# Turning u by transposing DMAs in place of TensorE transposes, in a fused attention and MLP kernel

## The chip, the core and the metric

The kernel runs on one core of a Trainium2 chip. The metric is the device time of one execution in microseconds (us); lower is better. The engines are named as in the profile: PE is TensorE (matmuls; its weight loads are listed as PEld), DVE is VectorE, ACT is ScalarE, POOL is GpSimd, SP is SyncE, which here only issues DMAs. POOL and ACT can issue DMAs as well.

## The reference

Inputs are q, k, v of shape (4, 8, 768, 64) and an 8x8 sort net per batch and head. After five rounds of normalising the sort net's rows and columns, keys and values are mixed between blocks of 96 tokens, attention runs inside each block, and a residual MLP of two stages follows on x (4, 768, 512):

```python
attn = softmax(scale * q_b @ k_sorted_b.T)          # inside each block
x = (attn @ v_sorted_b) as (batch, seq, 512)
a1 = alpha1 * x + beta1
tok = np.einsum('ts,bsd->btd', w_tok, a1)
u = x + lam * tok
a2 = alpha2 * u + beta2
ch = np.maximum(a2 @ w_ch1, 0.0) @ w_ch2            # 512 -> 2048 -> 512
return u + lam * ch
```

The change touches the line `a2 = alpha2 * u + beta2` and what feeds it.

## The kernel before

The order on every engine is written out by hand (`manual_schedule`); each engine runs its own instructions strictly in that order, and semaphores connect them. Per batch the 768 tokens are six tiles of 128 (kt 0 to 5), in two halves of three tiles (384 tokens). The 512 columns are four blocks of 128 (ci), the hidden 2048 are sixteen blocks (m).

`token_mix(b, kt)` does one token tile: six matmuls with the transposed `w_tok` into a psM bank (line 589), then u = x + rb on POOL (597), where rb is the row part (row sum of `w_tok` times beta1·lam), t = psum · alpha1·lam on DVE (601) and u += t on DVE (602). `row_part` (575 to 579) makes rb once, during batch 0: tile 0 on DVE, tile 1 on ACT, tiles 2 to 5 on POOL, one after each POOL u.

A copy of each u tile to bf16 (`u16`, ACT, line 603) is put in the list `late`; `tick()` runs such an entry at the second tick after it was entered, and `tick(True)` runs all at once. `weave` ticks once after each step of its main stream.

The channel MLP wants u with its columns on the partitions. `u_turn(b, half, ci)` (614 to 627) makes one of the 8 pieces per batch: three TensorE transposes of u16 into a PSUM bank (619), and an ACT activation that evicts it with alpha2 and beta2 as scale and bias (625) to a bf16 tile `a2T` [128, 384]. `hidden(b, half)` takes them: for each m four matmuls (635) and a relu, on DVE for every fourth m (643), else on ACT (645). `result(b, half, kk)` makes one output tile with sixteen matmuls (672), two DVE instructions (681, 682) and the store from SP (683).

PSUM: psM has three banks, shared by mixing, turns, hidden and result; psX has one (also used by a part of the turns); psA has two double banks for attention and for the preparation of keys, queries and values.

The stages for each batch b, n being the next batch: `both` is hidden(b, 0), three results of half 0 and hidden(b, 1), woven with `attention(n)`. `join` is, alternating, the mixing of batch n's tiles and the results of half 1 of batch b, woven with `ahead(n + 1)`, which prepares values (with a relay through DRAM, SP lines 412 and 418), queries and keys. The turns of half 0 of batch n stand between the matmuls of join's last result; the turns of half 1 stand in hidden(b, 0) after m = 5, 7, 9 and 11. Batch 0's mixing has a stage of its own, `opening`, with the four turns of half 0 inside. The last batch (b = 3) has no weaving, so no ticks.

Of the kernel before, what the change touches and what calls it, by code (L numbers as in the profile page):

```python
# [11 lines left out]
BF = mybir.dt.bfloat16  # L12
AF = mybir.ActivationFunctionType
ALU = mybir.AluOpType
# [5 lines left out]
def kernel(  # L20
# [24 lines left out]
    CT = C // 128  # L45
    HT = HID // 128
# [4 lines left out]
    TOK = S // 2  # L51
    scale = 1.0 / (D ** 0.5)
# [4 lines left out]
    psM = ctx.enter_context(tc.tile_pool(name="psM", bufs=3, space=bass.MemoryType.PSUM))  # L57
    psX = ctx.enter_context(tc.tile_pool(name="psX", bufs=1, space=bass.MemoryType.PSUM))
# [3 lines left out]
    def wt(shape, dtype, name):  # L62
        return wts.tile(shape, dtype, name=name, tag=name)
# [4 lines left out]
    def tmp(shape, dtype, name, bufs):  # L68
        return work.tile(shape, dtype, name=name, tag=name, bufs=bufs)
# [4 lines left out]
    def bank(pool, dtype=FT):  # L74
        n = 512 if dtype is FT else 1024
        tag = "psM" if pool is psM else "psX"
        return pool.tile([128, n], dtype, name=tag, tag=tag)

    V, A, PE, G, SP = nc.vector, nc.scalar, nc.tensor, nc.gpsimd, nc.sync
# [21 lines left out]
    u = {}  # L101
    u16 = wt([128, NT, C], BF, "u16")
    w_tokT = wt([128, NT, S], BF, "w_tokT")
    W1 = wt([128, CT, HID], BF, "W1")
# [76 lines left out]
    identbf = wt([128, 128], BF, "identbf")  # L181
# [79 lines left out]
    cols2 = wt([128, 2, CT], FT, "cols2")  # L261
# [37 lines left out]
    def row_sums():  # L299
        rs = bank(psM)  # L300
        for kt in range(NT):
            for ks in range(NT):
                PE.matmul(
                    rs[:, kt * 2:kt * 2 + 1], w_tokT[:, ks, kt * 128:(kt + 1) * 128],
                    ones_bf[:], start=(ks == 0), stop=(ks == NT - 1),
                )
        V.tensor_copy(
            rowsum[:], rs[:, 0:2 * NT].rearrange("p (k two) -> p k two", two=2)[:, :, 0]
        )
# [265 lines left out]
    def row_part(kt, eng):  # L575
        if eng is A:
            A.activation(rb[:, kt], b1lB[:], AF.Identity, scale=rowsum[:, kt:kt + 1])
        else:
            eng.tensor_scalar(rb[:, kt], b1lB[:], rowsum[:, kt:kt + 1], None, op0=ALU.mult)  # L579

    a2T_of = {}

    def token_mix(b, kt):
        if kt == 0:
            u[b] = tmp([128, NT, C], FT, "u", 2)
        x, ub = x16[b % 2], u[b]
        ps = bank(psM)
        for ks in range(NT):
            PE.matmul(  # L589
                ps[:], w_tokT[:, ks, kt * 128:(kt + 1) * 128], x[:, ks, :],  # L590
                start=(ks == 0), stop=(ks == NT - 1),
            )
        if b == 0 and kt == 0:
            row_sums()
            row_part(0, V)
            row_part(1, A)
        G.tensor_tensor(ub[:, kt], x[:, kt], rb[:, kt], ALU.add)  # L597
        if b == 0 and kt < NT - 2:
            row_part(kt + 2, G)
        t = tmp([128, C], FT, "tmix", 3)  # L600
        V.tensor_tensor(t[:], ps[:], a1lB[:], ALU.mult)  # L601
        V.tensor_tensor(ub[:, kt], ub[:, kt], t[:], ALU.add)  # L602
        late.append([2, lambda: A.copy(u16[:, kt], ub[:, kt])])  # L603

    late = []

    def tick(all_of_them=False):
        for item in list(late):
            item[0] -= 1
            if item[0] <= 0 or all_of_them:  # L610
                late.remove(item)
                item[1]()

    def u_turn(b, half, ci):
        if half == 0 or ci == 0:
            tick(True)
        ps = bank(psX if half == 0 and ci % 2 else psM, BF)
        for kk in range(3):
            PE.transpose(  # L619
                ps[:, kk * 128:(kk + 1) * 128],  # L620
                u16[:, half * 3 + kk, ci * 128:(ci + 1) * 128], identbf[:],
            )
        t = tmp([128, TOK], BF, "a2T", 9)
        a2T_of[b, half, ci] = t
        A.activation(  # L625
            t[:], ps[:, 0:TOK], AF.Identity, bias=cols2[:, 1, ci:ci + 1], scale=cols2[:, 0, ci:ci + 1]
        )

    hT_of = {}
# [1 line left out]
    def hidden(b, half):  # L631
        for m in range(HT):
            ps = bank(psM)
            for ci in range(CT):
                PE.matmul(  # L635
                    ps[:, 0:TOK], W1[:, ci, m * 128:(m + 1) * 128], a2T_of[b, half, ci][:],
                    start=(ci == 0), stop=(ci == CT - 1),
                )
            if m % 2 == 0:
                pair = tmp([128, S], BF, "hT", 10)  # L640
            t = hT_of[m] = pair[:, m % 2 * TOK:(m % 2 + 1) * TOK]
            if m % 4 == 3:
                V.tensor_scalar(t, ps[:, 0:TOK], 0.0, None, op0=ALU.max)  # L643
            else:
                A.activation(t, ps[:, 0:TOK], AF.Relu)  # L645
            if half == 0 and m in (5, 7, 9, 11):
                u_turn(b, 1, (m - 5) // 2)
            yield 0.65

    def last_result(b):  # L650
        kt = NT - 1
        for c in (slice(0, C // 2), slice(C // 2, C)):
            ps = bank(psM)
            for m in range(HT):
                PE.matmul(
                    ps[:, 0:C // 2], hT_of[m][:, 256:384], W2[:, m, c],
                    start=(m == 0), stop=(m == HT - 1),
                )
            t = tmp([128, C], FT, "tmix", 3)
            V.tensor_tensor(t[:, c], ps[:, 0:C // 2], lamB[:, c], ALU.mult)  # L660
            V.tensor_tensor(u[b][:, kt, c], u[b][:, kt, c], t[:, c], ALU.add)
            SP.dma_start(out[b, kt * 128:(kt + 1) * 128, c], u[b][:, kt, c])

    def result(b, half, kk, turn=None):
        kt = half * 3 + kk
        if b == B - 1 and kt == NT - 1:
            last_result(b)
            return
        ub = u[b]
        ps = bank(psM)  # L670
        for m in range(HT):
            PE.matmul(  # L672
                ps[:], hT_of[m][:, kk * 128:(kk + 1) * 128], W2[:, m, :],
                start=(m == 0), stop=(m == HT - 1),
            )
            if m % 4 == 3 and m < HT - 1:
                if turn is not None:
                    u_turn(turn, 0, m // 4)
                yield 0.86
        t = tmp([128, C], FT, "tmix", 3)  # L680
        V.tensor_tensor(t[:], ps[:], lamB[:], ALU.mult)  # L681
        V.tensor_tensor(ub[:, kt], ub[:, kt], t[:], ALU.add)  # L682
        SP.dma_start(out[b, kt * 128:(kt + 1) * 128, :], ub[:, kt])
        if turn is not None:
            u_turn(turn, 0, CT - 1)
        yield 0.86

    def mixing(b, kts):
        for kt in kts:
            token_mix(b, kt)  # L690
            yield 1.3
# [85 lines left out]
    first = ahead(1)  # L777
    next(first)
    token_mix(0, 0)
    next(first)  # L780

    def opening():
        yield from mixing(0, (1, 2, 3))
        u_turn(0, 0, 0)
        u_turn(0, 0, 1)
        yield 0.4
        yield from mixing(0, (4,))
        u_turn(0, 0, 2)
        u_turn(0, 0, 3)
        yield 0.4  # L790
        yield from mixing(0, (5,))

    weave(opening(), first, 0.8)
    load_k(2)
    load_q(2)
    load_v(2)
    for b in range(B):
        n = b + 1
        if n == B:
            for half in range(2):  # L800
                for _ in hidden(b, half):
                    pass
                for kk in range(3):
                    for _ in result(b, half, kk):
                        pass
            break

        def both(b=b):
            yield from hidden(b, 0)
            for kk in range(3):  # L810
                yield from result(b, 0, kk)
            yield from hidden(b, 1)
# [3 lines left out]
        def join(b=b, n=n):  # L816
            yield from mixing(n, (0,))
            yield from result(b, 1, 0)
            yield from mixing(n, (1, 2))
            yield from result(b, 1, 1)  # L820
            yield from mixing(n, (3, 4))
            yield from result(b, 1, 2, n)
            yield from mixing(n, (5,))
# [36 lines left out]
```

## Time and profile before

| | |
|---|---|
| median of 3 runs | 297.47 us (297.2 to 297.64) |
| the profiled execution | 297.77 us, of which the span is 295.9 |
| PE busy | 278.2 us (94%) |
| DVE busy | 170.2 us (58%) |
| ACT busy | 143.3 us (48%) |
| POOL busy | 71.9 us (24%) |
| transposes of u on PE (line 619) | 96 in 32 turns |
| evictions with the affine (line 625, ACT) | 32, 0.67 us each |
| copies of u to bf16 (line 603, ACT) | 24, 0.62 us each |
| DMA traffic | 27.09 MB, mean 92 GB/s |

Times in views count from the start of the span. A group's line gives, after the shapes, busy us and mean ns of one; after the second bar the engine's idle time just before them and what ended most of it. The chain of waits lists, in order of time, start, length and work of what ended last. The duration of a matmul in a group is from its issue to its modelled end, so the pace of several in a row is shorter than the sum of their durations.

The stages in this execution: opening from about 42 to 58 us; hidden, half 0, of batches 0, 1, 2 and 3 from 58.8, 123.5, 188.5 and 248.5 us; joins from about 99.7, 164.8 and 229.7 us.

### The profile page before, as it was taken

Reading aid. Unit: us, or ns where it says so; the run is one execution under the profiler, and the core shown is the slowest. Engines: PE = TensorE matmul, PEld = TensorE weight load, DVE = VectorE, ACT = ScalarE, POOL = GpSimd, SP = SyncE. Lnnn points to the kernel's source line nnn. Section 1 sums busy time; section 2 is a strip of 40 time slices with the busy share of each in tenths; the row PEclk is TensorE's granted clock in tenths of the full one; section 3 lists DMA queues with packets and bytes.
Section 4 is the critical chain, followed back from the end, with each engine's and each line's share of the span. In section 5 each row is a group of like instructions: output and inputs, shape, how many; then the busy total and the mean of one; then the engine's idle time right before and its main releaser. Section 6 shows DMA issues by size and latency. Waiting matters only on the chain.

```text
span 295.9 us, 7069 instructions
## 1 busy us (share of the span) xinstructions
PE 278.2 (94%) x3059; PEld 166.4 (56%) x3078; DVE 170.2 (58%) x315; ACT 143.3 (48%) x244; POOL 71.9 (24%) x86
## 2 busy tenths in 40 slices
PE   8968997799999999999999999999999999899994
PEld 6647854365556555565566455565566445545643
DVE  7887756885262669594452679592444684123224
ACT  3285857665436446664246455664344126811500
POOL 8399549910000532200000810000000900000000
PEclk9985999999999999999999999999999999999999
DMA  6997999999610039990110049100110010002012
GB/s 115 210 225 156 186 212 229 215 216 214 85 52 24 0 127 113 198 205 3 38 71 2 1 134 126 64 0 2 63 48 1 2 71 35 0 2 81 25 38 72
DMA packets 32135, 27.09 MB, mean 92 GB/s; under 512 B 19724, under 2 KB 26920, under 8 KB 32040
## 3 DMA queue, kind: packets, MB, share of 16 engines
q0 software_dynamic: 8976, 14.81, 28.4%
q1 hardware_dynamic: 23128, 11.82, 18.2%
q8 instruction: 24, 0.39, 0.5%
q14 instruction: 7, 0.06, 0.1%
HBM read 32.79 MB, written 8.65 MB: 140 GB/s over the span
## 4 chain that ended last, share of the span: by engine, by line
PE 75%; DVE 9%; POOL 5%; DMA 4%; ACT 4%; issue 1%; DVEq 0%; POOLq 0%
PE psM L635 28%; PE psM L672 23%; PE psM L589 7%; DMA u<-in_v_dram 4%; PE psA L516 3%; PE psA L490 2%; DVE kT L151 2%; PE psA L430 2%; PE psA L497 2%; DVE u L602 2%; POOL rb L579 2%; ACT a2T L625 2%; POOL u L597 2%; DVE x L529 1%; DVE mx L435 1%
## 5 line engine op out<-in xcount | busy, mean ns | idle before, releaser
L635 PE MATMUL psM<-a2T,W 128*128 128x384 bf16 x512 | 90.8, 326 | 0.9 <-ACT a2T L625 0.7
L672 PE MATMUL psM<-W,hT 128*128 128x512 bf16 x349 | 83.9, 379 | 1.6 <-issue 1.0
L645 ACT ACTIVATE hT<-psM 128x384 bf16<-128x384 f32 x96 | 46.5, 491 | 50.4 <-PE psM L635 49.1
L635 PEld LDWEIGHTS <-W 128*128 128x128 bf16 x512 | 47.8, 98 | 32.5 <-issue 2.3
L597 POOL TENSOR_TENSOR u<-x,rb 128x512 f32<-128x512 f16 x24 | 28.5, 1214 | 142.6 <-DVE x L529 140.7
L672 PEld LDWEIGHTS <-hT 128*128 128x128 bf16 x368 | 34.2, 98 | 37.2
L681 DVE TENSOR_TENSOR tmix<-psM,lamB 128x512 f32<-128x512 f32 x23 | 15.9, 690 | 39.4 <-PE psM L672 39.3
L643 DVE TENSOR_SCALAR hT<-psM 128x384 bf16<-128x384 f32 x32 | 17.7, 553 | 31.6 <-PE psM L635 27.2
L589 PE MATMUL psM<-x,w_tokT 128*128 128x512 f16 x144 | 34.7, 379 | 0.6 <-DVE x L529 0.6
L502 ACT ACTIVATE ET<-psA 96x768 f16<-96x768 f32 x28 | 21.1, 803 | 28.0 <-PE psA L497 28.0
L435 DVE TENSOR_REDUCE mx<-psA 96x8 f32<-96x768 f32 x30 | 27.3, 948 | 3.9 <-PE psA L430 3.7
L603 ACT CAST u<-u 128x512 bf16<-128x512 f32 x24 | 14.8, 618 | 21.9 <-DVE u L602 21.8
L602 DVE TENSOR_TENSOR u<-u,tmix 128x512 f32<-128x512 f32 x24 | 20.3, 846 | 6.5 <-POOL u L597 4.5
L589 PEld LDWEIGHTS <-w_tokT 128*128 128x128 bf16 x144 | 13.4, 98 | 15.3 <-DVE x L529 1.1
L601 DVE TENSOR_TENSOR tmix<-psM,a1lB 128x512 f32<-128x512 f32 x24 | 16.4, 683 | 3.1 <-PE psM L589 3.0
L625 ACT ACTIVATE a2T<-psM,cols 128x384 bf16<-128x384 bf16 x24 | 16.1, 670 | 3.4 <-PE psM L619 3.4
L682 DVE TENSOR_TENSOR u<-u,tmix 128x512 f32<-128x512 f32 x23 | 16.9, 734 | 1.5
L529 DVE TENSOR_TENSOR x<-psA,recip 128x768 f16<-128x768 f32 x16 | 15.3, 957 | 0.6
L490 PEld LDWEIGHTS <-kT 64*128 64x128 f16 x256 | 12.3, 98 | 5.2 <-issue 5.1
L490 PE MATMUL psA<-qT,kT 64*128 64x96 f16 x256 | 15.1, 212 | 0.2 <-ACT ET L502 0.2
L497 PE MATMUL psA<-tp,nmask 64*128 64x96 bf16 x256 | 15.0, 211 | 0.0
L528 DVE RECIPROCAL recip<-psA 128x12 f32<-128x12 f32 x16 | 3.7, 229 | 19.1 <-PE psA L516 19.1
(121 smaller groups left out, 295.1 us busy)
## 6 DMA issues: line engine op xcount, KB each, us to landing
out_dram<-u SPq DMA_DIRECT2D x23, 256.0 KB
W<-in_moe_w_ch_dram POOLq DMA_DIRECT2D x8, 512.0 KB, 20.2
rawk<-in_k_dram POOLq DMA_DIRECT2D x8, 384.0 KB, 7.6
qn<-in_q_dram POOLq DMA_DIRECT2D x8, 384.0 KB, 9.1
rawv<-in_v_dram POOLq DMA_DIRECT2D x6, 384.0 KB, 13.6
vscr<-rawv SPq DMA_DIRECT2D x3, 768.0 KB
vS<-vscr SPq DMA_DIRECT2D x8, 192.0 KB
hT<-in_moe_w_tok_dram POOLq DMA_DIRECT2D x6, 192.0 KB, 13.4
```

The lines of the kernel that those rows point to most:

```text
L435: V.tensor_reduce(mx[b % 2][:, :, c:c + 4], ps[0:BLK, :, 0:4 * BLK].rearrange("p l (i t) -> p l i t", t=BLK), AXX, ALU.max,)
L490: PE.matmul(ps[:, hl, i * BLK:(i + 1) * BLK], kT[r, p * S + c:p * S + c + 128], qT[b % 2][p][r, c:c + BLK], start=True, stop=False, skip_g ...
L497: PE.matmul(ps[:, hl, i * BLK:(i + 1) * BLK], nmask[r, n:n + 1].to_broadcast([64, 128]), tp_of[p][r, :], start=False, stop=True, skip_grou ...
L502: A.activation(exps(b, p)[:, :, g * 4:(g + 1) * 4, 0:BLK], ps[0:BLK, :, 0:4 * BLK].rearrange("p l (i t) -> p l i t", t=BLK), AF.Exp, scale ...
L529: V.tensor_tensor(x16[b % 2][:].rearrange("p s (l h d) -> p l s h d", l=2, d=D)[:, :, :, p], xg[:, :, :, 0:D], recip[:].unsqueeze(3).to_br ...
L589: PE.matmul(ps[:], w_tokT[:, ks, kt * 128:(kt + 1) * 128], x[:, ks, :], start=(ks == 0), stop=(ks == NT - 1),)
L597: G.tensor_tensor(ub[:, kt], x[:, kt], rb[:, kt], ALU.add)
L602: V.tensor_tensor(ub[:, kt], ub[:, kt], t[:], ALU.add)
L625: A.activation(t[:], ps[:, 0:TOK], AF.Identity, bias=cols2[:, 1, ci:ci + 1], scale=cols2[:, 0, ci:ci + 1])
L635: PE.matmul(ps[:, 0:TOK], W1[:, ci, m * 128:(m + 1) * 128], a2T_of[b, half, ci][:], start=(ci == 0), stop=(ci == CT - 1),)
L645: A.activation(t, ps[:, 0:TOK], AF.Relu)
L672: PE.matmul(ps[:], hT_of[m][:, kk * 128:(kk + 1) * 128], W2[:, m, :], start=(m == 0), stop=(m == HT - 1),)
```

## The change

The three transposes and the evicting activation of a turn go. In their place ACT, behind each bf16 copy of a u tile, issues one DMA that transposes the tile (128 tokens x 512 columns) into `a2T`, now one tile [128, 4, 384] for a half of a batch, with two buffers. The scale and bias are applied in place by one DVE instruction per column block (`affine`). The copies keep their place in the `late` list. The affines of half 0 stand where the turns stood; in the opening all four follow tile 4. The affines of half 1 move from m = 5, 7, 9, 11 to m = 12 to 15 of hidden(b, 0). Row parts 1 to 5 of batch 0 go to DVE.

```diff
             row_part(0, V)
-            row_part(1, A)
+            row_part(1, V)
         G.tensor_tensor(ub[:, kt], x[:, kt], rb[:, kt], ALU.add)
         if b == 0 and kt < NT - 2:
-            row_part(kt + 2, G)
+            row_part(kt + 2, V)
...
-        late.append([2, lambda: A.copy(u16[:, kt], ub[:, kt])])
+        late.append([2, lambda: u_turn(b, kt)])
...
-    def u_turn(b, half, ci):
-        if half == 0 or ci == 0:
+    def u_turn(b, kt):
+        half, kk = kt // 3, kt % 3
+        if kk == 0:
+            a2T_of[b, half] = tmp([128, CT, TOK], BF, "a2T", 2)
+        A.copy(u16[:, kt], u[b][:, kt])
+        A.dma_start_transpose(
+            a2T_of[b, half][:, :, kk * 128:(kk + 1) * 128], u16[:, kt, :]
+        )
+
+    def affine(b, half, ci):
+        if ci == 0:
             tick(True)
-        ps = bank(psX if half == 0 and ci % 2 else psM, BF)
-        for kk in range(3):
-            PE.transpose(
-                ps[:, kk * 128:(kk + 1) * 128],
-                u16[:, half * 3 + kk, ci * 128:(ci + 1) * 128], identbf[:],
-            )
-        t = tmp([128, TOK], BF, "a2T", 9)
-        a2T_of[b, half, ci] = t
-        A.activation(
-            t[:], ps[:, 0:TOK], AF.Identity, bias=cols2[:, 1, ci:ci + 1], scale=cols2[:, 0, ci:ci + 1]
+        t = a2T_of[b, half][:, ci, :]
+        V.tensor_scalar(
+            t, t, cols2[:, 0, ci:ci + 1], cols2[:, 1, ci:ci + 1], op0=ALU.mult, op1=ALU.add
         )
...
-            if half == 0 and m in (5, 7, 9, 11):
-                u_turn(b, 1, (m - 5) // 2)
+            if half == 0 and m >= HT - CT:
+                affine(b, 1, m - HT + CT)
...
                 if turn is not None:
-                    u_turn(turn, 0, m // 4)
+                    affine(turn, 0, m // 4)
...
         if turn is not None:
-            u_turn(turn, 0, CT - 1)
+            affine(turn, 0, CT - 1)
...
     def opening():
-        yield from mixing(0, (1, 2, 3))
-        u_turn(0, 0, 0)
-        u_turn(0, 0, 1)
-        yield 0.4
-        yield from mixing(0, (4,))
-        u_turn(0, 0, 2)
-        u_turn(0, 0, 3)
-        yield 0.4
+        yield from mixing(0, (1, 2, 3, 4))
+        for ci in range(CT):
+            affine(0, 0, ci)
         yield from mixing(0, (5,))
```

More of the change, by code (lines that the diff above doesn't have):

```diff
@@ L635, in hidden @@
                 PE.matmul(
-                    ps[:, 0:TOK], W1[:, ci, m * 128:(m + 1) * 128], a2T_of[b, half, ci][:],
+                    ps[:, 0:TOK], W1[:, ci, m * 128:(m + 1) * 128], a2T_of[b, half][:, ci, :],
                     start=(ci == 0), stop=(ci == CT - 1),
```

## The prediction

> **What bounds the kernel now.** First the page's busy times and slices, to see which engine is full and when. TensorE (PE) is busy 278.2 of 295.9 us.
>
> ```profile
> PE   8968997799999999999999999999999999899994
> DVE  7887756885262669594452679592444684123224
> ACT  3285857665436446664246455664344126811500
> PEclk9985999999999999999999999999999999999999
> DMA  6997999999610039990110049100110010002012
> ```
>
> From slice 8 on (59 us) PE is at nine tenths or more nearly to the end; slices 6 and 7 (44 to 59 us) are its last weak ones. The granted clock is full there, so nothing is to be had or lost from it. The DMA row is the warning: the engines are full through the first 75 us and again around 104 to 133 us. Second, windows (length, then busy us and instructions of PE, weight loads, DVE, ACT, POOL; clock; DMA share; GB/s):
>
> ```profile
> 44.00:52.00 8.00, 6.25 (x130) 3.88 (x130) 4.85 (x6) 5.79 (x9) 8.00 (x7) 1.00 1.05 231
> 52.00:60.00 8.00, 5.84 (x65) 3.25 (x64) 6.63 (x7) 5.08 (x9) 8.00 (x10) 1.00 1.30 212
> 60.00:70.20 10.20, 10.09 (x121) 6.18 (x120) 8.78 (x14) 6.30 (x14) 0.09 (x1) 1.00 1.35 218
> 99.70:123.30 23.60, 23.12 (x173) 11.95 (x174) 17.42 (x24) 13.62 (x21) 10.34 (x12) 1.00 0.73 118
> 248.40:261.00 12.60, 11.62 (x78) 7.05 (x77) 3.19 (x7) 8.87 (x17) 0.00 (x0) 1.00 0.06 22
> ```
>
> In the opening (44 to 60) PE idles 3.9 us and GpSimd (POOL) never: it alternates u (1.15 us) with row parts. In the first half of a hidden layer (60 to 70.2) and in a join (99.7 to 123.3) PE is the full engine. Third, the chain of waits, for what one turn costs PE, and the groups of the parts that go:
>
> ```profile
> 69.45 0.68 ACT a2T L625
> ...
> 121.83 0.33 PE psX L619 x3
> ...
> 128.04 0.32 PE psM L619 x3
> ```
> ```profile
> L619 PE MATMUL psM<-identbf,u 128*128 128x128 bf16 x72 | 8.3, 219 | 1.3 <-ACT u L603 1.3
> L625 ACT ACTIVATE a2T<-psM,cols 128x384 bf16<-128x384 bf16 x24 | 16.1, 670 | 3.4 <-PE psM L619 3.4
> L579 POOL TENSOR_SCALAR rb<-b1lB,rowsum 128x512 f32<-128x512 f32 x4 | 6.8, 1689 | 0.0
> L643 DVE TENSOR_SCALAR hT<-psM 128x384 bf16<-128x384 f32 x32 | 17.7, 553 | 31.6 <-PE psM L635 27.2 <-PE psX L461 4.5
> ```
>
> A turn (three transposes) moves the next matmul by 0.33 us; its group's mean of 219 ns is latency, not pace.
>
> **What the change takes off PE.** There are 32 turns (4 batches x 2 halves x 4 column blocks). The four of batch 0's first half lie in the opening, where PE has idle time; the other 28 stand in a full PE: 28 x 0.33 = 9.24 us. ACT loses 32 evictions of 0.67 us (21.4 us); ACT bounds no stage, so nothing is counted for it.
>
> **Where VectorE takes part of this back.** In the first hidden half of batches 0 to 2, four turns (1.32 us) go from PE, but the score maxima (eight of 0.95 us) and relus run on DVE almost without a pause: between 61.28 and 70.18 the timeline has one real gap, 0.75 us, spent waiting for the fourth pair of scores. DVE can end that stretch only 0.75 us earlier, and PE then waits for the relu of m=11, which stands behind the maxima. Loss 3 x (1.32 - 0.75) = 1.71 us.
>
> **The new affine on DVE.** 32 instructions of 128x384, bf16 to bf16. Not in this trace; below, the smallest casts (96x64 at 0.18 us); above, the relu of the same shape from PSUM (0.55). I take 0.3, nearer the small one because neither side is fp32 or PSUM. In the hidden stage they stand behind the last maximum, before the relu of m=15, whose result PE wants 15 matmuls (3.2 us) later: free, and at 0.55 each still under that. In a join three run behind u of token tile 4; the fourth waits for L681 and L682 of the last result (0.69 + 0.69), while PE has the mixing of tile 5 (1.30) and three of the first four hidden matmuls (0.49): 1.79 against about 1.7, so free, 0.3 us a join at the upper end.
>
> **The DMA itself.** 24 transposing DMAs of 128 KB, issued from ACT's queue, each behind its own copy to bf16 (0.62 us, L603, already there). Two costs are not in this trace.
> Issue time on ACT: below, SyncE's plain stores of u at 0.33 us; above, the relay into vS with its short rows, 5.75 us for four (1.44 each). I take 0.8. Queued behind it: in hidden stages, tile 5's DMA stands after the relu of m=0, so the relus of m=1 and 2 come later and PE, with three psM banks, stops at m=4 for 0.3 to 1.2 us; part of that DVE's paced stretch hides. I take 0.3 x 3 = 0.9 us. In joins, copies of kT and qT wait behind it for psA's two banks: 0.2 x 3 = 0.6 us (0 to 1.5 in all).
> Landing: below, the last store, also 128 KB on a hardware queue: u is ready at 292.88 and the span ends at 295.9, so at most 3.0 us with the end of the program in it. Above, with full DMA engines, the relay's first leg (vscr, 768 KB): issued 45.24, its successor starts at 53.45, 8.2 us. I take 3 us with quiet engines and 5 with full ones.
> In the opening tile 2's u ends by 50.2 on DVE (42.2, three row parts of 0.48, then tiles of 1.2 to 2.4 us), its copy at 50.9, the DMA is away at 51.7 and lands at 56.7. DVE gets to the affines at 55.9 (tiles 3 and 4, two kT copies of 1.21), so hidden starts near 57.9, against 58.3 (58.77 less the three matmuls done early): gain 0.5. In the join to batch 1 tile 2's copy ends at 113.83 and DVE reaches the affine at 119.87: 6.0 us for issue and landing, 5.8 by my values. The last join has 240.26 to 244.69 (4.4), with quiet engines 3.8. Both just fit.
>
> **Row parts.** Five of 0.48 us go to DVE (2.4 us, up to 1.2 each while POOL works, as L602 shows with 1.18 against 0.69); POOL loses 6.8 us, its u of tile 3 comes some 5 us earlier, and the opening's chain passes from POOL to DVE, ACT's copy and the DMA. The 0.5 us above is what that is worth.
>
> **Last batch.** Its hidden stage has no weaving, so tile 5's copy and DMA come only at m=12: relu at 9.15 us after the stage's start, copy 9.8, issue 10.6, landing 13.6, three affines, relu of m=15 at 15.1. PE wants that relu at 13.64: it waits 1.4 us. Before, this stage stood still for 12.6 - 10.4 - 1.3 = 0.9 us (for copy and eviction). Loss 0.5 (gain 0.4 to loss 3, by issue and landing).
>
> **Sum.** -9.24 + 1.71 + 0.9 + 0.6 - 0.5 + 0.5 = -6.0 us. The profiled execution took 297.77 (span 295.9 and 1.87 around it): 291.7; the shown runs' median is 0.3 lower: **291.4 us**. With both costs at their better ends (and the opening 2 us better) it is 287, with issue at 1.44 us 295.
>
> The Trainium skill speaks against the change: "VectorE: DVE Perf Modes", section "The three transpose paths", gives 1309 ns for a 128x128 tile through the DMA crossbar and 390 ns on TensorE. Four tiles one after another make 5.2 us (an estimate from that page) and, by the steps under rival B, about 295 us; no run here shows it yet.
>
> **Rivals.**
> *A. ACT is held in the issue (slower).* SyncE's own queue shows it:
>
> ```profile
> 53.45 13.28 SPq L418 DMA_DIRECT2D vS<-vscr  x2
> 109.09 5.75 SPq L418 DMA_DIRECT2D vS<-vscr  x4
> ```
>
> Two relay DMAs kept SyncE until 66.7 where the engines were full. If hardware queues share what fills up, tile 3's DMA (about 53.5) keeps ACT as long: no relus, and PE stops three banks after 58: about 7 us. In the joins to batches 1 and 2 ACT would be kept until 114.85 and its like; its kT copies hold psA, some 2.5 us each. -6.0 + 7 + 5 = +6: 303 us. It decides from 6 us of holds in all. For it: these rows. Against: they are that queue's own descriptors, 6144 short rows.
> *B. Transposes land late (slower).* The affine is in order on DVE, so a late one holds everything behind it. With 7 us to land, everywhere, it comes later than in the forecast by 2.0 in the opening (51.7 + 7 + four affines of 0.3 = 59.9 against 57.9), by 1.6 in each of the joins to batches 1 and 2 (DVE has it at 121.6, then 0.9 + 1.4 + 0.3 for three affines, the two instructions of the result and the fourth affine: 124.2 against 122.6), by 3.1 in the last join (likewise 250.7 against 247.6), by 4 in the last batch: 12.3 - 6.0 = +6.3, 304 us. Break-even is near 5.8 us. For it: full DMA engines. Against: the 3.0 us store.
> *C. Nothing gives back (faster still).* DVE's stretch doesn't pace, issue is at 0.3 us: 9.24 + 1.5 (the two 0.75 us stalls of the kind at 69.45) + 1.5 = 12: 285 us. Against it: DVE 8.78 of 10.2 us busy.
> That the change doesn't do what it says is excluded by the instruction order: no turns of u are left on PE.
>
> **Chances.** Forecast 0.56 (287 to 296), C 0.08, A 0.18, B 0.18. A measurement of this kernel tells 0.2%, 0.6 us, from no change. Nearly all of the first two is faster, 0.62; of A and B, whose sizes slide, a little falls within: 0.04; slower 0.34. The range leaves out half of C and the upper half of A and B: 286 to 304; the forecast's own is 287 to 296.
>
> **What would show it.** Right: no L619 or L625 rows, PE busy near 268 us, hidden's first half some 1 us shorter in batches 0 to 2, issue rows on ACT under 1 us, DVE's idle before the affine under 0.5 us each. A: long issue rows on ACT near 54 and 110 us with relus late behind them. B: DVE idle before the affine, released by a DMA. It would be wrong if either unknown lies above its upper row, or if the opening, where the DMA share is 1.3, starts hidden later than 60 us.

## The result: 5% slower, and the profile after

The changed kernel takes 313.38 us (median of 4 runs, 311.8 to 318.2), the kernel before 297.56 (4 runs, 297.2 to 297.87): a ratio of 1.050, 95% interval 1.045 to 1.055. The profiled execution of the changed kernel took 318.2 us (span 316.4) and is the longest of its runs; a second profile, at 313.8 us (the last experiment below), shows the same two waits in batch 0 and a smaller loss in batch 1 (1.8 us there, 4.8 in the table below).

The page after: span, the slices that were shown of before (one is 7.9 us), the DMA queues (packets, MB, share of 16 engines), and the chain by engine.

```profile
span 316.4 us, 6943 instructions
...
PE   8868995568589999998799999989999999989994
...
DVE  7886868356324356988524456988434477424223
ACT  3376764113212634553331644634435312420510
...
PEclk9985997767969999999989999999999999999998
DMA  6997999999941102999601004960010013101001
...
q0 software_dynamic: 8976, 14.81, 28.6%
q1 hardware_dynamic: 23128, 11.82, 17.9%
q10 hardware_dynamic: 13056, 3.15, 7.3%
...
PE 54%; DMA 21%; DVE 12%; ACT 5%; ACTq 3%; POOL 2%; issue 2%; DVEq 0%; POOLq 0%
```

PE, full from slice 8 on before, now has a hole in slices 6, 7, 8 and 10 (47 to 87 us), and in slices 7, 8 and 10 VectorE and ACT are nearly as empty: all three wait for something else. The DMA row is at nine in every one of these slices. The granted clock falls to 6 or 7 tenths in most of them. A queue q10 is new: 13,056 packets for 24 transposes, 544 each. On the chain DMA has gone from 4% to 21% and PE from 75% to 54%.

The groups of the new affine and of the hidden matmuls: after the first bar busy us and mean ns of one, after the second the idle time before them and what ended it.

```profile
L637 PE MATMUL psM<-a2T,W 128*128 128x384 bf16 x512 | 92.5, 333 | 10.4 <-DVE a2T L627 6.8
...
L627 DVE TENSOR_SCALAR a2T<-a2T,cols 128x384 bf16<-128x384 bf16 x32 | 10.8, 373 | 18.1 <-DMA a2T<-u 18.1
```

The affine itself is cheap. VectorE stood still for 18.1 us in front of it, and a DMA ended every bit of that. PE in turn waited for the affine, and (through work held behind it on VectorE) for more. Where the 18.1 us lie, the chain of waits tells: start, length and work.

```profile
43.36 1.30 DVE rb L579
...
49.37 0.63 ACT u L618
...
50.02 1.23 ACTq L619
...
51.29 0.29 ACT qT L149
...
52.79 0.53 ACT u L618
...
53.34 11.35 DMA a2T<-u
...
64.81 1.25 DVE a2T L627 x4
...
68.14 18.80 DMA a2T<-u
...
87.07 0.38 DVE a2T L627
```
```profile
133.50 5.26 DMA a2T<-u
...
138.84 0.96 DVE a2T L627 x3
...
143.49 13.01 DMA a2T<-u
...
156.53 0.38 DVE a2T L627
...
202.26 5.00 DMA a2T<-u
```

Five transposes are on this chain: tile 2 of batches 0, 1 and 2 (the last tile of half 0; 11.4, 5.3 and 5.0 us from issue to landing) and tile 5 of batches 0 and 1 (the last of half 1; 18.8 and 13.0 us). From the first matmul of each stage on PE, the two traces compare so (us; "hidden, half 0" ends with the first matmul of the results of half 0; "rest" is those results and hidden, half 1, up to the next join; the last rest goes to the end of the span; starts are rounded to 0.1 us before they are subtracted):

| stage | before | after | difference |
|---|---|---|---|
| up to the first hidden matmul | 57.2 | 65.2 | +8.0 |
| batch 0: hidden, half 0 / rest | 15.0 / 27.4 | 22.7 / 29.7 | +7.7 / +2.3 |
| join, then batch 1: hidden / rest | 23.7 / 13.9 / 27.5 | 22.6 / 17.2 / 29.0 | -1.1 / +3.3 / +1.5 |
| join, then batch 2: hidden / rest | 23.7 / 13.7 / 27.4 | 22.6 / 14.8 / 27.5 | -1.1 / +1.1 / +0.1 |
| join, then batch 3: hidden / rest | 18.8 / 12.3 / 35.3 | 18.2 / 11.6 / 35.3 | -0.6 / -0.7 / 0 |

The sum is 20.5 us, the difference of the spans. The joins and the last batch give what was hoped for; nearly all of the loss is from 47 to 100 us and from 140 to 186 us. The windows of the first of these stretches (length; busy us and instructions of PE, weight loads, VectorE, ACT, POOL; granted clock; DMA share; GB/s):

```profile
52.00:59.00 7.00, 6.16 (x75) 3.22 (x75) 5.03 (x6) 3.46 (x6) 2.28 (x4) 0.53 1.27 193
59.00:65.20 6.20, 0.47 (x3) 0.10 (x1) 0.63 (x3) 0.00 (x0) 2.59 (x4) 0.74 1.25 202
80.00:88.00 8.00, 3.60 (x24) 1.96 (x23) 3.07 (x7) 1.57 (x4) 0.00 (x0) 0.87 1.32 139
88.10:96.00 7.90, 7.90 (x84) 3.85 (x82) 2.31 (x6) 2.32 (x4) 0.00 (x0) 0.71 0.25 24
88.10:117.80 29.70, 29.70 (x338) 17.28 (x336) 11.45 (x21) 11.68 (x20) 0.56 (x1) 0.92 0.14 34
```

The second row is the wait for tile 2 (PE busy 0.47 of 6.2 us), the third the wait for tile 5; both with the DMA engines full. The fourth is a stage that waits for nothing, in which PE is busy all the time, at a clock of 0.71.

### The profile page after: what moved, and what is told of

It reads as the page before. It is cut to its first block, busy times and chain, and to the rows that moved or that the text cites. A ratio compares the mean times of both kernels' runs of the same rounds, so it can differ in the third digit from the quotient of the medians.

```text
span 316.4 us, 6943 instructions
## 1 busy us (share of the span) xinstructions
PE 283.7 (90%) x2982; PEld 163.1 (52%) x2982; DVE 182.8 (58%) x352; ACT 123.8 (39%) x211; POOL 66.0 (21%) x82
## 3 DMA queue, kind: packets, MB, share of 16 engines
q0 software_dynamic: 8976, 14.81, 28.6%
q10 hardware_dynamic: 13056, 3.15, 7.3%
## 4 chain that ended last, share of the span: by engine, by line
PE 54%; DMA 21%; DVE 12%; ACT 5%; ACTq 3%; POOL 2%; issue 2%; DVEq 0%; POOLq 0%
PE psM L674 20%; PE psM L637 18%; DMA a2T<-u 17%; DMA u<-in_v_dram 4%; PE psM L589 4%; PE psA L516 3%; ACTq L619 3%; PE psA L490 3%; ACT u L618 2%; DVE u L602 2%; PE psA L497 2%; DVE tmix L601 2%; DVE a2T L627 1%; ACT kT L149 1%; DVE x L529 1%
## 5 line engine op out<-in xcount | busy, mean ns | idle before, releaser
L637 PE MATMUL psM<-a2T,W 128*128 128x384 bf16 x512 | 92.5, 333 | 10.4 <-DVE a2T L627 6.8
L674 PE MATMUL psM<-W,hT 128*128 128x512 bf16 x368 | 88.1, 390 | 0.9 <-ACT hT L647 0.9
L637 PEld LDWEIGHTS <-W 128*128 128x128 bf16 x512 | 49.0, 99 | 45.5 <-issue 15.5
L597 POOL TENSOR_TENSOR u<-x,rb 128x512 f32<-128x512 f16 x24 | 29.3, 1246 | 165.8 <-DVE x L529 161.1
L674 PEld LDWEIGHTS <-hT 128*128 128x128 bf16 x368 | 35.2, 100 | 42.1 <-issue 4.4
L589 PE MATMUL psM<-x,w_tokT 128*128 128x512 f16 x144 | 36.5, 394 | 0.6 <-DVE x L529 0.6
L683 DVE TENSOR_TENSOR tmix<-psM,lamB 128x512 f32<-128x512 f32 x23 | 15.8, 689 | 35.9 <-PE psM L674 35.9
L645 DVE TENSOR_SCALAR hT<-psM 128x384 bf16<-128x384 f32 x32 | 17.7, 553 | 23.5 <-PE psM L637 22.6
L627 DVE TENSOR_SCALAR a2T<-a2T,cols 128x384 bf16<-128x384 bf16 x32 | 10.8, 373 | 18.1 <-DMA a2T<-u 18.1
L601 DVE TENSOR_TENSOR tmix<-psM,a1lB 128x512 f32<-128x512 f32 x24 | 16.4, 683 | 3.8 <-PE psM L589 3.8
L490 PE MATMUL psA<-qT,kT 64*128 64x96 f16 x256 | 16.2, 219 | 0.0
L490 PEld LDWEIGHTS <-kT 64*128 64x128 f16 x256 | 13.1, 102 | 5.8 <-issue 5.6
L497 PE MATMUL psA<-tp,nmask 64*128 64x96 bf16 x256 | 16.0, 218 | 0.0
L529 DVE TENSOR_TENSOR x<-psA,recip 128x768 f16<-128x768 f32 x16 | 15.3, 957 | 0.6
```

The source lines that it names most:

```text
L490: PE.matmul(ps[:, hl, i * BLK:(i + 1) * BLK], kT[r, p * S + c:p * S + c + 128], qT[b % 2][p][r, c:c + BLK], start=True, stop=False, skip_g ...
L497: PE.matmul(ps[:, hl, i * BLK:(i + 1) * BLK], nmask[r, n:n + 1].to_broadcast([64, 128]), tp_of[p][r, :], start=False, stop=True, skip_grou ...
L589: PE.matmul(ps[:], w_tokT[:, ks, kt * 128:(kt + 1) * 128], x[:, ks, :], start=(ks == 0), stop=(ks == NT - 1),)
L637: PE.matmul(ps[:, 0:TOK], W1[:, ci, m * 128:(m + 1) * 128], a2T_of[b, half][:, ci, :], start=(ci == 0), stop=(ci == CT - 1),)
L674: PE.matmul(ps[:], hT_of[m][:, kk * 128:(kk + 1) * 128], W2[:, m, :], start=(m == 0), stop=(m == HT - 1),)
```

## The experiments

Two theories stood first. By *landing*, transposes that are issued while the engines carry loads come late, and VectorE, which runs in order, is held at the affine. By *work*, VectorE and ACT simply have more to do than they had room for (affines, issues, row parts). Ratios are to the kernel before, on the same chip, with 95% intervals; spans are those of the profiled executions.

**Row parts alone.** The kernel before, with nothing but the row parts moved:

```diff
-            row_part(1, A)
+            row_part(1, V)
...
-            row_part(kt + 2, G)
+            row_part(kt + 2, V)
```

> The kernel before with nothing changed but row parts 1 to 5 of batch 0 on DVE. If the row parts on DVE relieve POOL as the prediction had it: 0.5 to 2 us faster than before. If DVE pays for them (1.38 us each beside POOL in the changed kernel's trace): no change or up to 1 us slower. In no case do they explain the 16 us.

297.05 us, 0.997 (0.9945 to 0.9996). On its own this part of the change is a small gain, so it does not explain the loss.

**Affines of half 1 put off**, from hidden's last four m into the last result of half 0, some 10 us later:

```diff
-            if half == 0 and m >= HT - CT:
-                affine(b, 1, m - HT + CT)
+            if half == 0 and m == HT - CT:
+                tick(True)
...
-                yield from result(b, 0, kk)
+                yield from result(b, 0, kk, (b, 1) if kk == 2 else None)
```

> The affines of half 1 are moved from m = 12 to 15 of hidden(b, 0) to the last result of half 0, some 8 us later; the copies and DMAs stay where they are. Theory (the DMAs land late because the DMA engines are full, and the loss is DVE held in order behind the affine): hidden's first half goes back from 22.7 to about 14 us in batch 0 and from 16.5 to about 13.5 in batch 1, the opening stays 7 us late: about 302 us. Rival (what costs is ACT's time in the 1.2 us issues, or the transposes share something with matmuls): the hidden stages hardly move, 310 us or more.

310.94 us, 1.042 (1.036 to 1.047). Hidden, half 0, went from 22.7 us (20.6 in the second profile of the changed kernel) to 15.3 in batch 0 and from 17.2 (15.7) to 15.0 in batch 1. In batch 0 holding VectorE for tile 5 was thus most of the stage's loss; before, the two stages took 15.0 and 13.9 us. The total still missed its forecast of 302 us. The opening is late as foreseen (hidden begins at 64.3), but the rest of batch 0 still takes 29.5 us, and not for the clock, which is 1.00 there: the relay of batch 1's values has landed only at 88.8, and PE waits for it:

```profile
88.83 0.92 PE L516 MATMUL psA<-vS,ET 96*128 96x65 f16 x24 [1.15 <-DMA vS<-vscr]
```

And the fourth affine, now behind the two VectorE instructions of a result, comes late for the next stage: the rests of batches 1 and 2 are 28.2 instead of 27.4 us, the last one 36.8 instead of 35.3.

**Batch 0 back on TensorE**, its turns and evictions at their old places, the other batches as changed:

```diff
-        A.dma_start_transpose(
-            a2T_of[b, half][:, :, kk * 128:(kk + 1) * 128], u16[:, kt, :]
-        )
+        if not on_pe(b, half):
+            A.dma_start_transpose(
+                a2T_of[b, half][:, :, kk * 128:(kk + 1) * 128], u16[:, kt, :]
+            )
+
+    def on_pe(b, half):
+        return b == 0
...
```

> Both halves of batch 0 are turned on TensorE as before, batches 1 to 3 by DMA. Theory (batch 0's DMAs meet full engines, later ones much less): the opening's 7 us, hidden(0, 0)'s 9 us and the lower clock after them go, what is left is a loss of some 2 us in batch 1's hidden and gains of 0.5 to 1 us in the other stages: 294 to 297 us. Rival (the transposes are slow wherever they stand): over 300 us.

302.02 us, 1.012 (1.008 to 1.017). The losses of the opening and of batch 0 are gone (hidden begins at 57.3, 14.6 and 27.4 us follow), so they belong to batch 0's transposes. The total is above 300 us, as the rival had it, but the stages do not bear the rival out: batches 2 and 3 are as in the changed kernel, and what is left of the loss is batch 1, with 18.2 us for hidden, half 0, and 29.1 for its rest, more than the 2 us expected. Two windows from there:

```profile
138.00:140.00 2.00, 0.00 (x0) 0.00 (x0) 0.73 (x4) 0.00 (x0) 0.00 (x0) 1.00 0.60 225
140.00:150.00 10.00, 9.97 (x107) 4.84 (x108) 2.81 (x7) 3.01 (x4) 0.00 (x0) 0.83 0.07 28
```

PE stands for 2.2 us until tile 5's affine (issued 126.04, reached by VectorE at 139.24), and the 10 us after it run at a clock of 0.83.

**The clock.** The rest of batch 0 has no wait of its own, yet takes 2.3 us longer. To see whether the wait ahead of it is the cause, matmuls of no use were put into the changed kernel's waits, 26 ahead of the first hidden stage and 20 behind m = 15:

```diff
+            if b == 0 and half == 0 and m == HT - 1:
+                dense(20)
...
         yield from mixing(0, (5,))
+        dense(26)
```

> The changed kernel with matmuls without use on TensorE where it waits for batch 0's DMAs (26 before hidden(0, 0), 20 after its m = 15). Theory of the clock (the granted clock fell to 0.64 in the wait and 0.92 in the 30 us after it because TensorE stood idle): the clock stays near 1.0 and the stage behind the wait goes from 29.7 back to 27.6 us; 2 to 4 us faster than the changed kernel, if the fill is no longer than the wait. Rival (the clock falls for another reason): clock and time as in the changed kernel, or some us slower.

318.21 us, 1.063 (1.057 to 1.070). No time came back. The first fill ended at 65.4, but tile 2 landed only at 69.9 in this run (issued 54.62), so PE stood for another 5.1 us, with a clock of 0.50 over the five us behind that; the second fill lasted 1.6 us longer than the wait. But the stage behind the second wait, which was filled to its end, is clean:

```profile
90.50:117.90 27.40, 27.40 (x337) 16.43 (x337) 10.52 (x18) 11.64 (x20) 0.36 (x1) 1.00 0.08 30
```

The same work in 27.4 us at a clock of 1.00, against 29.7 at 0.92 (27.4 / 0.92 = 29.8). So the unfilled wait of 4.4 us cost its length and then the clock behind it. Not every wait does: in batch 1 of the same run PE stands for 3.1 us, until 159.00, and behind it the clock is full:

```profile
159.00:169.00 10.00, 10.00 (x124) 5.45 (x125) 3.92 (x10) 3.01 (x4) 0.00 (x0) 1.00 0.08 29
```

**What delays the transposes: batch 1.** Batch 0 on TensorE as above, and the loads of keys, queries and values of batch 3, which were issued from POOL at the end of the join, wait until tile 5 of batch 1 has landed:

```diff
+    def loads_behind_turn(b):
+        G.tensor_copy(gate[:], a2T_of[b, 1][:, 0, TOK - 1:TOK])
+        load_k(b + 2)
+        load_q(b + 2)
+        load_v(b + 2)
...
+            if half == 0 and b == 1 and m == HT - CT - 1:
+                loads_behind_turn(b)
...
-        if b + 3 < B:
-            load_k(b + 3)
-            load_q(b + 3)
-            load_v(b + 3)
```

> Batch 0 on TensorE as in the run with batch 0 turned there (302.0 us), and the loads of batch 3's k, q and v wait on GpSimd (a copy of one column of a2T) until tile 5 of batch 1 is transposed. Theory (loads from POOL's queue in the DMA engines make tile 5's transpose 13 us long): it lands within 4 us of its issue, hidden(1, 0) falls from 18.2 to about 15 us and the stage after it from 29.1 to 27.5 as the clock stays up: 296 to 298 us. Rival (what is late is the relay's tail or the transposes among themselves): hidden(1, 0) stays above 17 us, 301 us or more.

296.11 us, 0.994 (0.992 to 0.997): faster than before. POOL's gate shows when tile 5 has landed (start, us, engine, line; in brackets the idle time before it and what ended it):

```profile
124.12 1.21 ACTq L620 DMA_TRANSPOSE a2T<-u  x1
...
127.96 0.19 POOL L652 COPY gate<-a2T 128x1 bf16<-128x1 bf16 x1 [22.28 <-DMA a2T<-u]
```

3.8 us from the start of the issue, against 13.2 with the loads under way. Hidden, half 0, of batch 1 is 14.4 us instead of 18.2, and its rest 27.4 instead of 29.1. In batch 1 it is the loads.

**The same in batch 0**: the changed kernel, with only batch 2's loads held until tile 5 of batch 0 has landed.

```diff
+            if half == 0 and b == 0 and m == HT - CT - 1:
+                loads_behind_turn(b)
...
-    load_k(2)
-    load_q(2)
-    load_v(2)
```

> The changed kernel with nothing but batch 2's loads of k, q and v held on GpSimd until tile 5 of batch 0 is transposed; the relay into vS stays. If those loads make up most of tile 5's 18.8 us: the first hidden half of batch 0 falls from 22.7 to 16 to 18 us, the opening stays late (the weights' loads are issued before), 305 to 308 us. If the relay makes it up: it stays above 20 us, 311 us or more.

308.39 us, 1.033 (1.025 to 1.040). Tile 5 lands 6.2 us after its issue instead of 18.8, and hidden, half 0, of batch 0 goes from 22.7 to 15.6 us. The opening is as late as it was (hidden begins at 64.3). In the changed kernel those loads are issued from 57.9 us on, behind W2's on the same queue, and tile 2 is no faster without them (11.6 us, against 11.4 with them).

**What delays the opening.** Two other transfers run in it: SyncE's relay of batch 1's values into vS, and POOL's loads of W2. The changed kernel without the relay's second leg for batch 1, the one that is in the opening (vS is set to ones):

```diff
-        for th in range(2):
+        for th in range(2 if b > 1 else 0):
             for m in range(steps):
...
```

> The changed kernel without the two DMAs that write batch 1's values from DRAM into vS (that part of the computation is left out: batch 1's attention uses ones as values). If the relay's 6144 short rows hold the opening's transposes: tile 2 lands within 5 us of its issue, hidden(0, 0) starts near 59 in place of 65 and its first half is near 15 us: 298 to 302 us. If the loads from POOL's queue (weights, then k, q and v of batch 2) hold them: hidden(0, 0) starts after 62 and takes more than 18 us: 308 us or more.

Its runs took 305.6 to 316.1 us, too far apart for a ratio; the profiled one, 308.9. Tile 2 takes 7.8 us (57.54 to 65.36) instead of 11.4, tile 5 13.6 instead of 18.8. The whole opening ran some 4 us later in this run (tile 2 is issued at 57.54, not 53.34), so hidden begins at 65.8 all the same, and its first half takes 17.4 us. The relay has a part; a larger one remains without it. And with a quarter of W2:

```diff
-    for m4 in range(4):
+    for m4 in range(1):
...
```

> The changed kernel with only the first of the four loads of W2 (its quarter is used in place of the other three, so the result differs). If the weights' loads on POOL's queue hold the opening's tile 2 (11 us from issue to DVE's start): it takes 6 us or less and hidden(0, 0) starts by 61 us in place of 64 to 65. If it is the relay's two legs: still 9 us or more, hidden(0, 0) after 63 us.

306.84 us, 1.030 (1.027 to 1.033). Tile 2 takes 7.5 us (54.94 to 62.46), between the two expectations, and the relay goes faster too:

```profile
54.59 2.94 SPq L418 DMA_DIRECT2D vS<-vscr  x2
```

In the changed kernel that entry, the time for which SyncE is held, is 18.64 us long, before it was 13.28; in all versions without transposes in the opening it is 13.1 to 15.9, in the others with all loads 17.2 to 24.1, and with batch 2's loads held 12.18. So no single transfer is at fault: the relay, the loads and the transposes slow each other.

How they share the engines, the changed kernel's trace shows by its packets. These are the queue rows for 75 to 80 us:

```profile
q0 software_dynamic: 651, 0.55, 87.1%
q1 hardware_dynamic: 651, 0.08, 24.2%
q10 hardware_dynamic: 652, 0.16, 17.9%
```

While the loads (q0), the relay (q1) and the transposes (q10) all have work, each queue gets as many packets through as the others, however many bytes they hold. And within q10 the transposes go one after another. With its packets counted off in order of time, 544 to each, those of batch 0 are as follows (us); VectorE is released 0.7 us after the last packet of tile 2 so counted and 1.3 us after tile 5's, which fits this order:

| tile | issue starts | first packet starts | last packet ends |
|---|---|---|---|
| 0 | 47.41 | 51.95 | 56.63 |
| 1 | 50.02 | 56.64 | 60.21 |
| 2 | 53.34 | 60.22 | 64.02 |
| 3 | 56.25 | 64.01 | 71.99 |
| 4 | 58.79 | 71.97 | 77.15 |
| 5 | 68.14 | 77.14 | 85.61 |

Tile 2 has its first packet after 6.9 of its 11.4 us, behind tiles 0 and 1; tile 5 after 9.0 of its 18.8 us, behind tiles 3 and 4. Even tile 0, with nothing ahead of it in its queue, waits 4.5 us for its first packet; the last tile 5 of the kernel, on quiet engines, waits 1.2.

**Tile 5 later.** A version in which nobody waits for it, without touching the loads: batch 0 on TensorE, tile 5's copy and transpose put off to the start of the results, its affines into the last result of half 0.

```diff
-        late.append([2, lambda: u_turn(b, kt)])
+        late.append([2 if on_pe(b, kt // 3) or kt < NT - 1 else 99, lambda: u_turn(b, kt)])
...
+        if half == 0 and kk == 0:
+            tick(True)
...
```

> Batch 0 on TensorE (302.0 us); in batches 1 to 3 the copy and the transposing DMA of tile 5 go from behind the relu of m = 0 to behind hidden's first half, and the affines of half 1 to the last result of half 0. Theory (ACT's copy and issue, 0.62 + 1.21 us in order before the relus of m = 1 and 2, stop TensorE): hidden(2, 0) falls from 14.7 to about 13.2 us and hidden(3, 0) from 11.7 to 10.5; batch 1, where the loads still run, may be held in its last result instead. 296 to 300 us. Rival (the maxima on DVE set the pace of that stage, and ACT's issue is hidden): hidden(2, 0) stays at 14 us or more.

296.05 us, 0.994 (0.992 to 0.997). The hidden stage of the last batch, half 0, falls to 10.6 us as expected (nothing runs beside it). In batch 2 it is 14.4, not 13.2: there tile 5's transpose is no longer in the way, and VectorE still paces it. The fourth affine again comes late behind a result's instructions (rests of 28.2, 28.2 and 36.7 us).

**Both together**, with the fourth affine ahead of the result's two VectorE instructions:

```diff
                     affine(*turn, m // 4)
+                    if m // 4 == CT - 2 and not on_pe(*turn):
+                        affine(*turn, CT - 1)
```

> All together: batch 0 on TensorE, tile 5's copy and DMA behind hidden's first half, the affines of half 1 in the last result of half 0, batch 3's loads behind tile 5's transpose, and the fourth affine of a half ahead of the result's two DVE instructions. If late landing, ACT's issue and DVE's order are all of the loss, the stages of batches 1 to 3 come out at 13.2, 13.2 and 10.5 us for hidden's first half and 22.4, 22.4 and 17.6 for the joins, without falls of the clock: 290 to 293 us, faster than before. Rival (the transposes cost the rest of the kernel something else, such as slower loads or relays): 296 us or more.

292.71 us (292.36 to 293.31), 0.984 (0.981 to 0.986). This version beats both kernels. The total is where it was expected; hidden, half 0, of batches 1 and 2 is not (14.3 and 14.1 us in place of 13.2). Tile 5 of batch 1 lands in 2.5 us, now that it meets quiet engines:

```profile
136.85 1.22 ACTq L620 DMA_TRANSPOSE a2T<-u  x1
139.34 0.19 POOL L652 COPY gate<-a2T 128x1 bf16<-128x1 bf16 x1 [33.06 <-DMA a2T<-u]
```

What remains is at the start of hidden, half 0 (same version, timeline):

```profile
121.15 1.25 DVE L644 TENSOR_SCALAR a2T<-a2T,cols 128x384 bf16<-128x384 bf16 x4 [1.44 <-DMA a2T<-u]
...
123.05 0.81 PE L661 MATMUL psM<-a2T,W 128*128 128x384 bf16 x4 [0.25 <-DVE tmix L714]
...
124.38 0.81 PE L661 MATMUL psM<-a2T,W 128*128 128x384 bf16 x4 [0.52 <-DVE tmix L601]
```

Four affines, 1.25 us, stand on VectorE ahead of the two instructions that read PSUM banks (L714 of the last result, L601 of tile 5), and PE waits for these banks. VectorE itself stood for 1.44 us before them, until tile 2's transpose had landed.

**What the affine costs.** Two versions of the last one. Half 0's affines on ACT:

```diff
+        if half == 0:
+            A.activation(
+                t, t, AF.Identity, bias=cols2[:, 1, ci:ci + 1], scale=cols2[:, 0, ci:ci + 1]
+            )
+            return
```

> The combination (292.7 us) with the four affines of a half 0 on ACT in place of DVE. Theory (with late landing gone, what eats the turns' 2.6 us per batch in batches 1 and 2 is DVE: the affines stand before the instructions that free psM's banks and before the maxima): join and first hidden half together fall from 36.9 and 36.7 us to about 35.6: 290 to 291.5 us. Rival (ACT then waits in order for the transpose, and its relus come later): no gain, 292.5 us or more.

301.1 us, 1.009 (1.006 to 1.013). On ACT four take 2.50 us and stand behind copies and issues; join and hidden, half 0, of batch 1 take 39.9 us together, against 36.9. (1.3 us of the loss are not the affines': in the rest of batch 0 PE waits for the relay's values, as it did when the affines of half 1 were put off.) And without half 0's affines in batches 1 to 3:

```diff
+        if half == 0:
+            return
```

> The combination (292.7 us) with the affines of half 0 of batches 1 to 3 left out (that scale and bias are then missing in the result). If DVE's extra work there keeps batches 1 and 2 from showing the turns' 2.6 us: join and first hidden half together fall from 36.9 and 36.7 us to below 36, 290.5 to 291.5 us. If something else sets the pace (the maxima alone, or the scores' order): they stay above 36.4 us, 292 us or more.

290.74 us, 0.978 (0.976 to 0.981). Join and hidden, half 0, together: 35.8, 35.9 and 28.5 us for batches 1 to 3, against 36.9, 36.7 and 28.5. With the affines VectorE loses 1 us in each batch that has attention beside it and nothing in the last. The version does not tell whether that is their 1.25 us of work or the wait in front of them: without affines VectorE does not wait for the transpose either (1.44 and 1.13 us in batches 1 and 2 of the combination, none in batch 3). Folding alpha2 into the weights would take both off VectorE; it was not tried.

**The changed kernel once more**, unaltered, for a profile nearer to its median:

> The changed kernel once more, unaltered, for a second profile: 311 to 314 us, with the granted clock again below 0.8 in the opening's wait, tile 2 of batch 0 about 11 us and tile 5 about 18 us from issue to DVE's start.

313.82 us (span 312.0). The same two waits, for tile 2 (53.10 to 65.37, with its affines' start) and tile 5 (68.69 to 85.51); hidden begins at 65.8, and batch 0 takes 20.6 and 30.0 us, batch 1 15.7 and 27.4.

## Why the prediction was wrong

The sign was missed. It forecast 291.4 us with rival B, *transposes land late*, at 0.18; B is what happened, at 313.4 instead of the 304 it was priced at. One of the forecast's own signs of being wrong, a hidden stage that begins later than 60 us, is in the trace: it begins at 65.2.

**The step that failed** is "Landing: [...] I take 3 us with quiet engines and 5 with full ones". As the price of a transpose with nothing ahead of it in its queue it was fair, even a little high: the last tile 5, alone on quiet engines, is used 2.4 us after its issue starts (after, timeline):

```profile
279.32 1.21 ACTq L619 DMA_TRANSPOSE a2T<-u  x1
...
281.74 0.96 DVE L627 TENSOR_SCALAR a2T<-a2T,cols 128x384 bf16<-128x384 bf16 x3 [3.48 <-DMA a2T<-u]
```

and tile 2 of batches 1 and 2, with full engines, takes 5.3 and 5.0 us with its issue, where the forecast had 5.8. What it left out is that transposes queue behind each other, and that each is slowed by every queue beside it. In batch 0 they are issued 2.5 to 9.4 us apart, and the packets of one take 3.6 to 8.5 us there, where those of the last tile 5 take 0.9; each transpose begins where the one ahead of it ends. In batch 1 tiles 3, 4 and 5 take 4.1, 4.7 and 5.5 us, after a first packet 4.0 us behind tile 3's issue. Tile by tile the wait adds up, and the one that VectorE needs is the last. The bound above, 8.2 us for the relay's first leg, was the landing of a single transfer too, and so was no bound: 11.4, 13.0 and 18.8 us lie beyond it. B had the same fault, 7 us for each, wherever it stood, and its break-even point of 5.8 us was passed only in three places, but there by far.

That a packet of a transpose waits its turn with a packet of each other queue is what the equal counts above (651, 651, 652) show. It gives the size roughly. From the queue rows, a packet takes on average 0.286 x 316.4 x 16 / 8976 = 0.161 us on q0, likewise 0.039 on q1 and 0.028 on q10; one transpose has 544 / 16 = 34 packets per engine, and 34 x (0.161 + 0.039 + 0.028) = 7.8 us, an estimate at the upper end of the 3.6 to 8.5 seen. The Trainium skill, "DMA: Bandwidth & Descriptors", section "Queues, rings and completion order", says that an engine goes round the queues it has work for packet by packet; the trace agrees in these counts. Holding back the loads alone brought tile 5 from 13.2 to 3.8 us and from 18.8 to 6.2.

**Tile 5 of half 1 was not priced at all.** The affines of half 1 were called free because they "stand behind the last maximum, before the relu of m=15". That compared their length with PE's cover and took their input for granted. In batch 0 PE stood 4.4 us for it; of the 7.7 us that the stage lost, another 1.7 are the long issue of 3.40 us named below, and about as much is the low clock of its first twelve matmuls (3.83 us, 2.12 before). In batch 1 PE stood 2.1 us of the 3.3 for it. The versions that put these affines off or held the loads show 15.3 us in batch 0 and 14.4 in batch 1.

**The opening.** Forecast: tile 2's transpose issued at 50.9, landed at 56.7. It was issued at 53.34 and landed at 64.7: 2.4 us of the 8.0 late are the issue, 5.6 the landing (11.4 instead of 5.8), most of it behind tiles 0 and 1. The issue was late because ACT had two earlier issues (1.80 and 1.23 us, taken as 0.8) and two copies of qT ahead of tile 2's copy. PE, waiting for these copies, stood for 3.4 us:

```profile
52.84 1.07 PE L343 MATMUL psA<-PB,rawk 128*64 128x64 f16 x32 [3.42 <-ACT qT L149]
```

**The clock.** "The granted clock is full there, so nothing is to be had or lost from it" was true of before only. After those 3.4 us it was 0.53 for the next 7 us, and after the wait for tile 5 (4.4 us without matmuls) 0.71 for the next 8. The stages behind the waits took 2.3 us (batch 0) and 1.5 (batch 1) more than their work, 3.8 of the 20.5 us; in the second profile it was 2.6 and nothing. That the wait is the cause, the experiment with useless matmuls shows for batch 0, and the same stage takes 27.4 us in versions without the long wait. What a shorter wait brings is not certain: over all runs, from 40 us on, the clock was 0.50 to 0.65 in the five us behind each wait of PE's of 4.4 us or more; behind waits of 1.4 to 3.7 us it was 0.50 to 0.72 in some places and full in others. The Trainium skill, "TensorE: Matmul & The Clock Gate", section "Part 1: The HAM clock gate (the "warmup" mystery)", has the clock halved or full by how busy the array was in a window of some 3.4 us that runs freely; the 0.53 after 3.4 us agrees, and so do the mixed outcomes of the shorter waits.

**Issue and rival A.** An issue on ACT is 1.21 us (median of 24), half again the 0.8 taken, within the upper row of 1.44. Rival A, ACT held in the issue as SyncE is, came true once, for 3.40 us at 68.14, and stopped PE for 1.7 us. In batches 1 and 2 the relu behind the issue cost PE 0.88 and 0.99 us where 0.3 was taken. A is a small part of the loss.

**VectorE.** That it paces hidden, half 0, was right and still too mild. "In a join three run behind u of token tile 4 [...] so free" was wrong: without the affines, and the wait for their input, join and hidden are 1 us shorter in batches 1 and 2.

**What was right.** A turn is 0.33 us of PE: where nothing else paces, in the last join and hidden stage, the combination and the version without affines take 28.5 us against 31.1 before, 2.6 us for 8 turns. The last rest is unchanged, the row parts are a small gain (0.3%), the last batch's hidden stage is 0.7 us shorter where a change of 0.5 to the other side was taken. With batch 0 left on TensorE and the waits gone the kernel is 5.0 us faster than before (297.70 to 292.71); the forecast of 6.0 counted about 1 us for batch 0. That these agree so closely is partly luck, since this version's order is another than the one forecast. The gain of a turn was sized well, and the sum failed on the DMA.

## What to carry to other kernels

Price a DMA that an in-order engine waits for by the traffic of its moment and by the transfers ahead of it in its own queue, up to the last one needed, not by one landing; ask for every consumer, also the one whose work seems free, when its input lands. A transposing DMA pays where its consumer comes late or the loads can be held back for some microseconds, and in a stage with full engines the turn on TensorE, at 0.33 us, is the cheaper one. A wait of PE's can cost more than its length, since the next stage may run at a lower clock: here it did behind every wait of 4.4 us or more, and behind some of 1.4 to 3.7.

## What the runs showed of the hardware

- A transposing DMA of 128x512 bf16 from SBUF to SBUF has 544 packets. Alone it is ready 2.4 to 2.5 us after the start of its issue, of which ACT is held for 1.21; its packets take 0.9 us of that. In batch 0, beside loads and a relay, its packets take 3.6 to 8.5 us, and those of the next one begin only behind them.
- Three DMA queues with work at the same time got equal numbers of packets through (651, 651 and 652 in 5 us), though these carried 0.55, 0.08 and 0.16 MB.
- PE's granted clock fell already after a wait of 2.2 us: 0.83 over the 10 us behind it (batch 0 on TensorE, 140 to 150 us). After another of 3.1 us it stayed at 1.00 (useless matmuls, 159 to 169 us).
- Transfers of different queues slow each other more than their bytes suggest: the transposes add 3.1 MB to 27.1, and the relay's entry on SyncE's queue grew from 13.28 to 18.64 us; with 1.5 MB less of W2 it took 2.94.
- What stays open: why the first packet of a transpose came 4.0 and 4.5 us after its issue (tile 3 of batch 1, tile 0 of batch 0) where the engines were busy and its own queue was empty, against 1.2 on quiet engines, and whether transposes issued from SyncE's queue would fare otherwise (not tried).
